# Corner blocks alone by DMA in batch 0, the division by the row sums behind the product with v, and earlier products

## The chip, the core and the metric

The kernel runs on one core of one Trainium2 chip. TensorE (PE) multiplies matrices into PSUM, VectorE (DVE) and ScalarE (ACT) work on PSUM and SBUF, GpSimd (POOL) on SBUF, and 16 DMA engines move data; nearly all transfers are issued from SyncE's queue (SP). Each engine runs its own queue in order, and semaphores hold an instruction until what it needs is there. The metric is the device time of one execution in microseconds (us), the median of three runs.

## The reference

An attention block with a threshold, followed by a feed-forward block, all in float32:

```python
# q, k, v: (8 batches, 8 heads, 576, 64)
scores = q @ k.T / 8                       # per head, 576 x 576
scores = where(scores >= rowmax - tau, scores, -1e9)
attn = exp(scores - rowmax)
attn = attn / (rowsum(attn) + 1e-9)
x = (attn @ v) -> (8*576, 8*64)            # tokens x 512
h = x @ w_in                               # 4608 x 1024
e = exp(h - rowmax); sm = e / (rowsum(e) + 1e-9)
u = h * sm
ln = (u - mean(u)) / sqrt(var(u) + 1e-6) * g_ln
out = ln @ w_out                           # 4608 x 512
```

w_in and w_out arrive as 64-bit floating-point numbers; the kernel turns their bits into float32 itself.

## The kernel before, in words

**Slots and rounds.** The attention is cut into 144 slots, 18 to a batch (PER = 18). A slot (b, kind, hp, r) is 128 query rows for each of the two heads of pair hp, against all 576 keys. Kinds 0 and 1 are the first 512 queries; kind 2 takes the last 64 queries of all pairs. Slots with r = 0 and r = 1 belong together, and such a pair of slots is a *unit* with the key (b, kind, hp): slots 2n and 2n + 1. The loop at the end of the kernel runs one round for each slot (rnd), and in each round it writes out, by hand, the order of the work for every engine. The order in which an engine gets its instructions is the order of this text.

**A slot on its way.** In round s: PE computes the scores of both heads into PSUM (`scores`, L434). VectorE finds for each head the extreme of a row and adds tau (`maxes`, L455: one custom instruction and a short read of its accumulator, twice). ScalarE turns the scores into a value that is 0 or very far from it (`ramp`, L470, out of PSUM), which sets the PSUM free for the next slot, and then takes the exponential with its row sum `sm` (`exps`, L479). In round s + 1: GpSimd computes 1/(sum + 1e-9) (`normalise`, L486 and L487) and multiplies both heads' 128x576 by it (L489); VectorE transposes both in blocks of 32x32 (`blocks`, L501) into the unit's tile T. When the second slot of a unit is transposed, DMAs carry T into a second tile wT in which the 32-row blocks stand where the product needs them (L510 and L512, or L517 for kind 2): 1152 KB in three or four transfers.

**The product with v.** Some rounds later (`pv_due`: 3 after the second slot, LAG_PV, plus 1 for slots below 6 and slots 11, 17 and 27) PE multiplies wT with v (`attend_steps`, L542, 72 matmuls, into a pair of PSUM banks taken from the two pairs p0 and p1), and `attended` copies the result into xh or xe, the tokens of the feed-forward (L572, ScalarE). A product is only started in a round with no feed-forward step on PE or with an h step.

**The feed-forward** is cut into pieces of 128 tokens. A piece has two h steps (`ff_h`, L605 with `split`, 32 matmuls each), max and exponential (L620, L629), the multiplication h * e (L635), statistics (L650 and GpSimd's L654 to L661), normalisation to V and u (L671, L676), a swap of blocks by DMA (`ff_swap`, L687), a transposition (`ff_turn`, L697) and two o steps (`ff_o`, L710, 64 matmuls each). In `ff_o` the flag `other` says which of the two PSUM banks takes which rows of w_out. At most one step of this kind runs in a round.

**Weights.** In the first 16 rounds one 128x512 piece x of the weights is made each round, x = rnd + 1: `weight_load` (DMA into a raw tile), `weight_e` on ScalarE (L263), `weight_m` on VectorE (L282 multiplies the high words by 2^-112, L286 masks and shifts the result), `weight_b` on VectorE (L308), and one round later `weight_c` on GpSimd (L332), for pieces from 8 on also `weight_f` on ScalarE (L340) and `weight_d` (DMA, L347). In a round VectorE gets `weight_b(x)` and then `weight_m(x + 1)`.

**Heads.** For batch 0, q and k of a head pair are turned by PE (`turn`, L371) and kept in SBUF by ScalarE (`keep`: L388 for k, L390 for q). `whole_pair` does so for pairs 1, 2 and 3 in rounds 0, 2 and 4; it takes both PSUM pairs p0 and p1, q in the first. The columns of kT are written in an order that puts the even keys first.

**The order in a round**, as far as the change touches it: scores, maxes, ramp and exps of slot rnd; `whole_pair`; `normalise(rnd - 1)`; the feed-forward jobs in `middle`; `weight_c`; a feed-forward step on PE; the product with v (`attend_steps`, then `attended`); `blocks(rnd - 1)`; the jobs in `late`; `weight_e`, `weight_b`, `weight_load`, `weight_m`; `weight_f`, `weight_d`; loads of q, k and v.

**Buffers.** w has four buffers, T two, wT two; raw tiles of the weights share the places of the feed-forward's tiles.

## Time and profile before

| | |
|---|---|
| median of 3 runs | 856.63 us (856.11 to 857.89) |
| the profiled execution | span 854.9 us; the profile gives no time around it |
| PE, busy share of the span | 96% |
| VectorE | 79% |
| ScalarE | 67% |
| GpSimd | 58% |
| DMA, queue q1 | 165.82 MB, 76.7% of the 16 engines' span |

A line of the timeline has the start in us, the length in us, the engine, the line of the kernel, the operation, output and input tiles, the shape (partitions x elements) and how many instructions were merged (x2); in brackets at its end stands how long the engine was idle before it, and what ended that. Consecutive instructions of an engine overlap a little, so the step from one start to the next is the better measure of what an instruction costs in its queue. A line of a group has the line, engine, operation, tiles, shape and count, then the sum of busy time, the mean length in ns, and the idle time before. Lines of DMA give the count, the size of one and the median time from issue to landing.

### The profile page before, as it was taken

How to read it: one execution, taken by the hardware profiler on the slowest of the kernel's cores; microseconds unless marked ns; L12 is line 12 of the kernel's file. 1: busy time of each engine (PE TensorE's matmuls, PEld its weight loads, DVE VectorE, ACT ScalarE, POOL GpSimd, SP SyncE). 2: the span in 40 equal slices, each digit the busy share in tenths (PEclk: the TensorE clock that was granted, in tenths of full speed). 3: DMA queues.
4: the chain of work that ended last, by engine and by line, in shares of the span. 5: the costliest groups of instructions: out<-in, count | busy, mean ns of one | idle time of the engine just before them, and what ended most of it. 6: DMA issues, size and time to landing. Idle time of an engine off the chain costs nothing.

```text
span 854.9 us, 36109 instructions
## 1 busy us (share of the span) xinstructions
PE 819.9 (96%) x15363; PEld 620.5 (73%) x15363; DVE 674.6 (79%) x1225; ACT 570.0 (67%) x1127; POOL 496.1 (58%) x945
## 2 busy tenths in 40 slices
PE   6778899999999999999999999999999999999997
PEld 5555677778677787777688877777777777777655
DVE  5997787989788888888788878888888878787361
ACT  6886876777767666667666666666677777775121
POOL 4885656666566656565566666565666655555120
PEclk8899999999999999999999999999999999999999
DMA  9999778798888888887888778887788887655212
GB/s 343 254 249 213 191 194 233 188 259 204 226 229 202 211 185 218 216 216 190 201 215 218 195 177 209 207 217 207 195 221 226 207 188 175 165 137 140 67 38 63
DMA packets 75314, 168.54 MB, mean 197 GB/s; under 512 B 11146, under 2 KB 32658, under 8 KB 75154
## 3 DMA queue, kind: packets, MB, share of 16 engines
q1 hardware_dynamic: 74866, 165.82, 76.7%
q8 instruction: 120, 1.97, 1.0%
q10 hardware_dynamic: 288, 0.43, 0.2%
q14 instruction: 40, 0.33, 0.1%
HBM read 46.14 MB, written 9.44 MB: 65 GB/s over the span
## 4 chain that ended last, share of the span: by engine, by line
PE 83%; DMA 4%; DVE 4%; ACT 3%; issue 2%; POOL 2%; SPq 1%; DVEq 0%; ACTq 0%; POOLq 0%
PE o_ps L710 27%; PE h_ps L605 22%; PE s_ps L434 15%; PE pv L542 14%; DMA wT<-T 3%; PE h_ps L595 3%; ACT w L470 1%; DVE w L455 1%; ACT w L479 1%; DVE T L501 1%; POOL w L489 1%; POOL sm L487 0%; PE s_ps L379 0%; DVE w L308 0%; PE tp L371 0%
## 5 line engine op out<-in xcount | busy, mean ns | idle before, releaser
L710 PE MATMUL o_ps<-w,uT 64*64 64x256 f32 x4608 | 269.5, 376 | 2.2 <-issue 1.6
L470 ACT ACTIVATE w<-s_ps,nth 128x576 f32<-128x576 f32 x280 | 196.8, 738 | 105.6 <-DVE nth L455 88.6
L455 DVE CUSTOM_DVE_ANT_0 w<-s_ps,tau_t 128x576 f32<-128x576 f32 x280 | 200.0, 751 | 83.5 <-PE s_ps L434 52.4
L710 PEld LDWEIGHTS o_ps<-w,uT 64*64 64x64 f32 x4608 | 221.8, 133 | 55.4 <-ACT xh L572 12.0
L489 POOL TENSOR_SCALAR w<-w,sm 128x576 f32<-128x576 f32 x288 | 220.6, 778 | 14.3
L501 DVE STREAM_TRANSPOSE T<-w 128x576 f32<-128x576 f32 x288 | 207.7, 756 | 22.6 <-POOL w L489 22.3
L605 PE MATMUL h_ps<-w,xh 64*64 64x512 f32 x1856 | 220.8, 589 | 0.0
L479 ACT ACTIVATE w<-w,ntau 128x576 f32<-128x576 f32 x288 | 219.6, 767 | 0.0
L542 PEld LDWEIGHTS pv<-wT,v 64*64 64x64 f32 x5760 | 172.6, 136 | 39.8 <-issue 16.7
L434 PE MATMUL s_ps<-kT,qT 64*64 64x512 f32 (+1 forms) x2048 | 175.8, 416 | 13.4 <-ACT w L470 11.3
L542 PE MATMUL pv<-wT,v 64*64 64x128 f32 (+1 forms) x5760 | 173.9, 263 | 8.3 <-DMA wT<-T 7.4
L605 PEld LDWEIGHTS h_ps<-w,xh 64*64 64x64 f32 x1856 | 118.4, 133 | 77.2 <-issue 43.6
L486 POOL TENSOR_SCALAR sm<-sm 128x2 f32<-128x2 f32 x144 | 34.2, 237 | 186.5 <-ACT w L479 182.8
L487 POOL TENSOR_TENSOR sm<-sm,mone 128x2 f32<-128x2 f32 x144 | 106.7, 741 | 12.0
L434 PEld LDWEIGHTS s_ps<-kT,qT 64*64 64x64 f32 x2048 | 72.7, 137 | 21.7 <-ACT w L470 16.2
L572 ACT COPY xh<-pv 128x256 f32<-128x256 f32 x64 | 25.4, 396 | 80.9 <-PE pv L542 80.9
L671 ACT ACTIVATE V<-u,nb,rs 128x1024 f32<-128x1024 f32 x36 | 44.7, 1240 | 40.5 <-POOL nb L661 33.6
L697 DVE STREAM_TRANSPOSE uT<-V 128x1024 f32<-128x1024 f32 x36 | 44.1, 1225 | 15.9 <-DMA V<-u 15.6
L479 ACT ACTIVATION_READ_ACCUMULATOR w<-w,ntau 128x1 f32 x288 | 55.4, 192 | 0.0
L676 DVE TENSOR_SCALAR u<-u,rs,nb 128x1024 f32<-128x1024 f32 x36 | 34.9, 971 | 19.5 <-ACT V L671 17.9
L635 DVE TENSOR_TENSOR u<-h_ps,u 128x1024 f32<-128x1024 f32 x36 | 42.8, 1190 | 9.4 <-ACT u L629 9.4
L620 DVE TENSOR_REDUCE hm<-h_ps 128x1 f32<-128x1024 f32 x36 | 42.9, 1193 | 4.9 <-PE h_ps L595 2.7
(77 smaller groups left out, 553.5 us busy)
## 6 DMA issues: line engine op xcount, KB each, us to landing
wT<-T SPq DMA_DIRECT2D x160, 288.0 KB, 6.5
wT<-T SPq DMA_DIRECT2D x64, 576.0 KB, 5.5
v<-in_v_dram SPq DMA_DIRECT2D x16, 576.0 KB, 6.0
V<-u SPq DMA_DIRECT2D x144, 64.0 KB, 3.5
out_dram<-ob SPq DMA_DIRECT2D x71, 128.0 KB, 2.6
q<-in_q_dram SPq DMA_DIRECT2D x28, 288.0 KB, 6.1
k<-in_k_dram SPq DMA_DIRECT2D x27, 288.0 KB, 6.4
qT<-flip SPq DMA_DIRECT2D x48, 144.0 KB, 3.2
```

The source lines that it names most:

```text
L434: nc.tensor.matmul(out=ps[h][ROWS[y], ks], lhsT=lhsT, rhs=d["kT"][ROWS[h], ks], start=True, stop=True,)
L455: nc.vector.tensor_tensor_reduce(out=w, in0=ps[:, 0:S], in1=(zero if loose else tau_t).to_broadcast([P, S]), scale=1.0, scalar=BIG, op0=AL ...
L470: nc.scalar.activation(out=d["w"][x], in_=d["w"][x] if d["loose"] else d["ps"][x][:, 0:S], func=AF.Prelu, bias=d["nth"][x], scale=-1.0, al ...
L479: nc.scalar.activation(out=w, in_=w, func=AF.Exp, bias=ntau, scale=1.0, accum_out=sm[:, x : x + 1])
L487: nc.gpsimd.tensor_tensor(out=sm, in0=sm, in1=mone, op=ALU.pow)
L489: nc.gpsimd.tensor_scalar(out=w, in0=w, scalar1=sm[:, x : x + 1], scalar2=1.0, op0=ALU.mult, op1=ALU.mult)
L501: nc.vector.transpose(out=T[:, :, r, h, :], in_=w)
L542: nc.tensor.matmul(out=to, lhsT=d["v"][ROWS[u], (h0 + h - u) % 4, m,], rhs=rhs, start=m == 0, stop=m == NK - 1,)
L605: mm = nc.tensor.matmul(out=h[ROWS[y], f], lhsT=x[ROWS[r], c, ROWS[y]], rhs=w1_parts[ROWS[r], c, part ^ r], start=part == 0 and c == 0, st ...
L671: nc.scalar.activation(out=V, in_=u, func=AF.Identity, bias=nb, scale=rs)
L697: nc.vector.transpose(out=uT, in_=d["V"].rearrange("p y (m x) -> p m y x", x=32))
L710: nc.tensor.matmul(out=d["o"][ROWS[z], 512 * (r ^ other) : 512 * (r ^ other) + 256], lhsT=d["uT"][ROWS[r], m].rearrange("p y x -> p (y x)" ...
```

## The change

Seven edits, all of which touch batch 0 or the weights:

1. **`weight_s`** (new): for pieces 4 to 10 the multiplication by 2^-112 is made by GpSimd, into the place of the finished weight, two pieces ahead (in round x - 3 for piece x); `weight_m` then only masks and shifts.
2. **`keep`**: for the head pairs of batch 0, kT keeps the keys in their own order.
3. **`normalise`**: for slots below 18 it computes 1/(sum + 1e-9) but no longer multiplies the weights by it. `sm` of these slots lives in a tile with six buffers.
4. **`corners`** (new) takes the place of `blocks` for slots below 18: VectorE transposes into T in another order of blocks, GpSimd copies the slot's share of T (128x1152) into a second tile `more` (`copy`, called behind `weight_b`), and with the second slot of a unit four DMAs of 32 partitions bring the blocks that stand in the wrong 32 rows back from `more` into T, 590 KB in all. The product then reads T.
5. **`spread`** (new): at the end of a product of batch 0, eight small matmuls against the identity write 1/sum, one value for each query column and repeated over the 64 rows of a head, into PSUM beside the product; ScalarE copies them to SBUF (`by`, in the place of `more`).
6. **`attended`**: for batch 0 two VectorE multiplications of 128x128 (product in PSUM by `by`) write the tokens; ScalarE's copy L572 falls away there.
7. **When products run**: the extra round is left out for slots 1, 3, 5 and 11; in round 18 (rnd == PER) a product may run behind an o step. In `ff_o`, `other` is off for batch 0.

The core of the diff:

```diff
+    def weight_s(x):
+        if in_bits(x):
+            hi = raws[x]["raw"].bitcast(F32).rearrange("p (n two) -> p n two", two=2)[:, :, 1]
+            dst = piece(x)[1]
+            nc.gpsimd.tensor_scalar(
+                out=dst, in0=hi, scalar1=2.0**-112, scalar2=1.0, op0=ALU.mult, op1=ALU.mult
+            )
+            raws[x]["scaled"] = dst.bitcast(I32)
...
         if nm == "k":
+            if i < NP:
+                of, to = room[:, 0 : 64 * len(ms)], pair(i)["kT"][:, 64 * ms[0] : 64 * ms[-1] + 64]
...
         nc.gpsimd.tensor_tensor(out=sm, in0=sm, in1=mone, op=ALU.pow)
+        if s < PER:
+            return
...
+    def corners(s):
...
+        T, more = [u[x].rearrange("p (c m) r h x -> p c m r h x", c=2) for x in ("T", "more")]
+        for h, w in enumerate(d["w"]):
+            nc.vector.transpose(out=T[:, :, :, r, h], in_=w.rearrange("p (m c x) -> p c m x", m=NK, c=2))
+
+        def copy():
+            of, to = [u[x][:, :, r].rearrange("p k h x -> p k (h x)") for x in ("T", "more")]
+            nc.gpsimd.tensor_copy(out=to, in_=of)
+            if r == 0:
+                return
+            of, to = [x.rearrange("p c m r h x -> p c (m r h x)") for x in (more, T)]
+            for g in range(2):
+                for half in range(2):
+                    at, src = 64 * half + 32 * (1 - g), 64 * half + 32 * g
+                    nc.sync.dma_start(out=to[at : at + 32, g], in_=of[src : src + 32, 1 - g])
+            u["wT"] = T.rearrange("p g m r h x -> p g m r h x")
+
+        return copy
...
+    def spread(key):
...
+        for r, rc in enumerate(unit["rc"]):
+            for u in range(2):
+                for h in range(2):
...
+                    nc.tensor.matmul(
+                        out=to, lhsT=rc[ROWS[u], h : h + 1].to_broadcast([64, 64]),
+                        rhs=ident[ROWS[u], ROWS[u]].rearrange("p (g x) -> p g x", g=2), start=True, stop=True,
+                    )
...
+        nc.scalar.copy(out=by, in_=y)
...
     def attended(key):
         b, kind, hp = key
+        if b == 0:
+            spread(key)
+            by = units[key]["by"]
...
-        nc.scalar.copy(out=to, in_=y)
+        if b == 0:
+            for u in range(2):
+                nc.vector.tensor_tensor(out=to[:, u], in0=y[:, u], in1=view(by)[:, u], op=ALU.mult)
+        else:
+            nc.scalar.copy(out=to, in_=y)
...
-        other = len(t) == 3 and t[2]
+        other = len(t) == 3 and t[0] > 0 and t[2]
...
+    LATE = (PER - 1, PER + 9)
+    SCALED = range(4, 11)
...
-            pv_due.append((s + LAG_PV + (s < 6 or s in (11, PER - 1, PER + 9)), (b, kind, hp)))
+            pv_due.append((s + LAG_PV + (s in LATE), (b, kind, hp)))
...
-            if due and (step is None or step[0] == "h") and len(pairs_free) > (step == ("h", 0)):
+            if due and (step is None or step[0] == "h" or rnd == PER) and len(pairs_free) > (step == ("h", 0)):
...
-            if rnd - 1 in live:
+            copied = None
+            if rnd - 1 in live and rnd - 1 < PER:
+                copied = corners(rnd - 1)
+            elif rnd - 1 in live:
                 blocks(rnd - 1)
...
                 weight_b(x)
+                if copied is not None:
+                    copied()
+                    copied = None
...
                     weight_m(x + 1)
+                if x + 2 in SCALED:
+                    weight_s(x + 2)
+            if copied is not None:
+                copied()
```

More of the change, by code (lines that the diff above doesn't have):

```diff
@@ L281, in weight_m @@
         if in_bits(x):
[L282 to L287 removed]
+            of = d.get("scaled", m)
+            if of is m:
+                nc.vector.tensor_scalar(
+                    out=m.bitcast(F32), in0=hi.bitcast(F32), scalar1=2.0**-112, scalar2=None,
+                    op0=ALU.mult,
+                )
+            nc.vector.tensor_scalar(
+                out=m, in0=of, scalar1=0x7FFFFFFF, scalar2=3,
                 op0=ALU.bitwise_and, op1=ALU.logical_shift_left,
@@ L476, in exps @@
         d = live[s]
-        d["sm"] = sm = small.tile([P, 2], F32, tag="sm", name="sm")
+        d["sm"] = sm = small.tile(
+            [P, 2], F32, tag="late" if s < PER else "sm", bufs=6 if s < PER else 3, name="sm"
+        )
         for x, w in enumerate(d["w"]):
@@ L491, in normalise @@
             )
+    def corners(s):
+        b, kind, hp, r = slots[s]
+        key = (b, kind, hp)
+        if r == 0:
+            units[key] = dict(
+                T=work.tile([P, NB, 2, 2, 32], F32, tag="T", name="T"),
+                more=work.tile([P, NB, 2, 2, 32], F32, tag="wT", bufs=2, name="wT"),
+                rc=[],
+            )
+        u = units[key]
+        d = live.pop(s)
+        u["rc"].append(d["sm"])
+        T, more = [u[x].rearrange("p (c m) r h x -> p c m r h x", c=2) for x in ("T", "more")]
[4 more added lines that the diff above has]
+            nc.gpsimd.tensor_copy(out=to, in_=of)
+            if r == 0:
+                return
[6 more added lines that the diff above has]
+        return copy
     def blocks(s):
@@ L550, in attend_steps @@
                         yield
+    def spread(key):
+        b, kind, hp = key
+        unit = units[key]
+        y = unit["y"][1].rearrange("p (u n) -> p u n", u=2)[:, :, 256:384]
+        for r, rc in enumerate(unit["rc"]):
+            for u in range(2):
+                for h in range(2):
+                    to = y[ROWS[h], u]
+                    if kind == 2:
+                        to = to.rearrange("p (r g x) -> p r g x", r=2, g=2)[:, r]
+                    else:
+                        to = to.rearrange("p (g r x) -> p r g x", r=2, g=2)[:, r]
+                    nc.tensor.matmul(
+                        out=to, lhsT=rc[ROWS[u], h : h + 1].to_broadcast([64, 64]),
+                        rhs=ident[ROWS[u], ROWS[u]].rearrange("p (g x) -> p g x", g=2), start=True, stop=True,
+                    )
+        unit["by"] = by = unit["more"].rearrange("p k r h x -> p (k r h x)")[:, 0:256].rearrange(
+            "p (u n) -> p u n", u=2
+        )
+        nc.scalar.copy(out=by, in_=y)
     def attended(key):
         b, kind, hp = key
+        if b == 0:
+            spread(key)
+            by = units[key]["by"]
         tag, y = units.pop(key)["y"]
```

11 lines of the change are left out of this document (4 added, 7 removed).

## The prediction

> **What bounds the kernel now.** I read the page, then busy time by stretches, then the engines' instructions in order of time for the first 20 of the 144 rounds. Columns of a stretch: length, busy time (and count) of each engine, granted clock, DMA share, rate.
>
> ```profile
> span 854.9 us, 36109 instructions
> PE 819.9 (96%) x15363; PEld 620.5 (73%) x15363; DVE 674.6 (79%) x1225; ACT 570.0 (67%) x1127; POOL 496.1 (58%) x945
> ...
> 70.00:77.00 7.00, 3.84 (x80) 3.60 (x84) 3.44 (x4) 0.12 (x2) 4.36 (x7) 0.80 1.05 226
> 180.00:190.00 10.00, 10.00 (x176) 8.79 (x172) 8.45 (x17) 7.10 (x15) 5.57 (x12) 1.00 1.02 269
> ```
>
> From about 120 us PE is full (10.00 of 10), and it cannot catch up there. The change touches batch 0 only, so what counts is how much earlier or later round 30 starts, where the walk of the loop gives the same work as before. Here is round 7 on VectorE. Each round opens with the first of its two L455, and I call that moment M; counting pairs from round 0 gives M7 = 42.92 and M8 = 47.31.
>
> ```profile
> 42.92 0.75 DVE L455 CUSTOM_DVE_ANT_0 w<-s_ps,tau_t 128x576 f32<-128x576 f32 x1
> ...
> 44.28 1.43 DVE L501 STREAM_TRANSPOSE T<-w 128x576 f32<-128x576 f32 x2
> 45.64 0.83 DVE L308 SCALAR_TENSOR_TENSOR w<-raw,em 128x512 int32<-128x512 int32 x1
> 46.51 0.43 DVE L282 TENSOR_SCALAR em<-raw 128x512 f32<-128x512 f32 x1
> 46.97 0.43 DVE L286 TENSOR_SCALAR em<-em 128x512 int32<-128x512 int32 x1
> 47.31 0.75 DVE L455 CUSTOM_DVE_ANT_0 w<-s_ps,tau_t 128x576 f32<-128x576 f32 x1
> ```
>
> There is no gap: in rounds 4 to 11 VectorE is the bound, at 4.39 us in this round. Its own queue is the thing to watch. ScalarE in rounds 4, 7 and 16:
>
> ```profile
> 32.34 0.72 ACT L390 ACTIVATE qT<-tp,scl 128x576 f32<-128x576 f32 x1
> ...
> 46.62 0.38 ACT L572 COPY xh<-pv 128x256 f32<-128x256 f32 x1
> ...
> 101.74 0.39 ACT L572 COPY xh<-pv 128x256 f32<-128x256 f32 x1
> ```
>
> The copy of the product with v stands behind ramp and exps of its round; in round 7 it ends at 47.00, M + 4.08. Today nobody on VectorE waits for it.
>
> The third bound is the transfer of the transposed weights in round 12: in the chain of waits 12.33 us, while VectorE and ScalarE have next to nothing to do (70 to 77 us above).
>
> ```profile
> 61.22 12.33 DMA wT<-T
> ```
>
> **The change, part by part.** Edits counted from M of the round.
>
> *VectorE waits for ScalarE.* In batch 0 the last step of a product with v is now: 8 small matmuls (spread), a ScalarE copy of 128x256 in the place of L572, then two VectorE multiplications 128x128, and these stand in VectorE's queue ahead of the two transposes, L308, L286 and the next round's L455. The ScalarE copy has the size of L572, so it ends at M + 4.08 at the earliest, +0.07 to hand over. For the multiplications:
>
> ```profile
> 118.59 0.28 DVE L388 COPY kT<-s_ps 128x128 f32<-128x128 f32 x1
> 118.80 0.54 DVE L392 TENSOR_SCALAR qT<-s_ps,scl 128x320 f32<-128x320 f32 x1
> ...
> L635 DVE TENSOR_TENSOR u<-h_ps,u 128x1024 f32<-128x1024 f32 x3 | 3.6, 1188 | 0.0
> ```
>
> One costs between 0.15 (128/1024 of L635) and 0.28 (the copy of 128x128 out of PSUM, whole); I take that copy's 0.21 from start to start, 0.42 for two.
>
> The rounds as they are now (M4, M5, M11, M12, M13, M16, M17, M18 and M20 are the L455 rows, in this order):
>
> ```profile
> 28.64 0.76 DVE L455 CUSTOM_DVE_ANT_0 w<-s_ps,tau_t 128x576 f32<-128x576 f32 x1
> ...
> 33.41 0.75 DVE L455 CUSTOM_DVE_ANT_0 w<-s_ps,tau_t 128x576 f32<-128x576 f32 x1
> ...
> 61.98 0.76 DVE L455 CUSTOM_DVE_ANT_0 w<-s_ps,tau_t 128x576 f32<-128x576 f32 x1 [0.48 <-PE s_ps L434]
> 66.38 0.76 DVE L455 CUSTOM_DVE_ANT_0 w<-s_ps,tau_t 128x576 f32<-128x576 f32 x1
> 78.37 0.76 DVE L455 CUSTOM_DVE_ANT_0 w<-s_ps,tau_t 128x576 f32<-128x576 f32 x1 [4.86 <-PE s_ps L434]
> 97.45 0.76 DVE L455 CUSTOM_DVE_ANT_0 w<-s_ps,tau_t 128x576 f32<-128x576 f32 x1 [2.51 <-PE s_ps L434]
> ...
> 100.17 1.20 DVE L697 STREAM_TRANSPOSE uT<-V 128x1024 f32<-128x1024 f32 x1
> 101.30 1.19 DVE L620 TENSOR_REDUCE hm<-h_ps 128x1 f32<-128x1024 f32 x1
> 102.41 0.74 DVE L455 CUSTOM_DVE_ANT_0 w<-s_ps,tau_t 128x576 f32<-128x576 f32 x1
> ...
> 106.88 0.76 DVE L455 CUSTOM_DVE_ANT_0 w<-s_ps,tau_t 128x576 f32<-128x576 f32 x1 [0.43 <-PE s_ps L434]
> 117.24 0.75 DVE L455 CUSTOM_DVE_ANT_0 w<-s_ps,tau_t 128x576 f32<-128x576 f32 x1
> ```
>
> So the transposes start at M + 4.57 in place of M + 1.36: +3.21 in a round with such a product. The multiplication by 2^-112 (L282), 0.46 from start to start, leaves VectorE in rounds 2 to 8. Rounds 6 and 8 become 4.39 + 3.21 - 0.46 = 7.14, round 10 (not relieved) 7.60; rounds 5 and 7 become 3.93, round 9 stays 4.39. Together 34.1 where it is 61.98 - 33.41 = 28.6: **+5.6**.
>
> *The first product moves from round 5 to round 4*, where whole_pair(3) holds both PSUM pairs.
>
> ```profile
> 33.12 2.29 PE L542 MATMUL pv<-wT,v 64*64 64x128 f32 x72 [0.79 <-ACT qT L390]
> ```
>
> It waits for the same ScalarE copy as now, which ends at M4 + 4.42 (33.06 - 28.64), but this is now a wait in VectorE's round 4: product to M + 6.8, spread 0.25 (8 of 72 matmuls of the row), copy to 7.5, multiplications to 8.0, transposes, L308 and L286 2.6, so M5 = M4 + 10.6 in place of 4.77: **+5.8**.
>
> *Corners by DMA.* 590 KB a pair of slots in place of 1152, so the 12.33 us should go. But the SyncE transfer now follows the POOL copy, which follows the late transposes, with one round less of lag.
>
> ```profile
> L489 POOL TENSOR_SCALAR w<-w,sm 128x576 f32<-128x576 f32 x44 | 32.6, 754 | 2.2
> ...
> L487 POOL TENSOR_TENSOR sm<-sm,mone 128x2 f32<-128x2 f32 x22 | 16.9, 768 | 1.8
> L332 POOL TENSOR_TENSOR w<-w,em 128x512 int32<-128x512 int32 x11 | 14.6, 1329 | 6.0 <-DVE w L308 6.0
> ...
> L486 POOL TENSOR_SCALAR sm<-sm 128x2 f32<-128x2 f32 x22 | 6.1, 276 | 22.7 <-ACT w L479 22.0
> ```
>
> By the slope from L486 to L489, 0.83 ns a column, the copy of 1152 columns takes 1.23 us (between 0.96, without the fixed part, and 1.51, as two L489). From M of the round: transposes end 6.0, copy 7.4, the fourth of four issues starts 2.2 later (0.72 each), and lands 3.6 (as V<-u, also between SBUF tiles) to 8.1 us after (as the 144 KB loads): 13.2 to 17.7.
>
> ```profile
> L517 SPq DMA_DIRECT2D wT<-T x4: 567/720/1538, 111.1 to 114.0; - x4
> k<-in_k_dram SPq DMA_DIRECT2D x8, 144.0 KB, 8.1
> V<-u SPq DMA_DIRECT2D x8, 64.0 KB, 3.6
> ```
>
> The product of two rounds later is needed at M + 12.2 (M of its round is 11.07 later, and it must start 1.1 behind that to be ready for the ScalarE copy). So each of three products comes 1.0 to 5.5 late; I take 1.0, the row of the nearest kind: **+3.0** (up to +16).
>
> *Rounds 11 to 13.*
>
> ```profile
> 66.06 3.80 PE L605 MATMUL h_ps<-w,xh 64*64 64x512 f32 x32
> ...
> 106.67 3.63 PE L710 MATMUL o_ps<-w,uT 64*64 64x256 f32 x64
> ```
>
> Round 12 loses its DMA wait. VectorE opens it later than PE has its scores, so the h there (3.44 to the next matmul) ends at M + 2.35, the product at 4.55, spread and ScalarE copy 5.2, multiplications 5.7, then transposes, L620, L308, L282, L286: 9.8 in place of 78.37 - 66.38 = 12.0: **-2.2**. Rounds 13 to 15 I count at nothing, 1 either way: a product moves from round 15 to 14, and h in rounds 13 and 14 (3.44 each) covers VectorE's wait as far as it goes.
>
> *Rounds 16 and 17.* The ScalarE copy of round 16 ends at M + 4.7 (102.13 - 97.45; two keeps stand before it), the multiplications at 5.2, then by the rows L501 1.36, L697 1.13, L620 1.11: M17 = M16 + 8.8 where it was 4.96, and o of round 17 waits for L697 as now: **+3.8**.
>
> *Round 18 with its product behind o.* o (106.67 to 110.1) to M + 3.2, product 5.4, spread, copy, multiplications 6.5, transposes 7.9, M19 at 8.1. The round of the product alone (19) falls away, but the walk of the loop shows that rounds 27, 28 and 29 then carry products alone, not just 28 and 29: one round like round 7 more, 4.4. 12.5 for 117.24 - 106.88 = 10.4: **+2.1**.
>
> *Near nothing.* Transposes no longer waiting for POOL's scaling gain some 0.3 in rounds 1 to 3, where PE's scores are as late; contiguous kT, the swapped o banks and the product of slots 16 and 17 in round 23 (PE is full there; VectorE's wait is covered by 5 us of h and v) cost 0 to 1. POOL's round: 0.28 + 0.77 + 1.33 + 1.23 + 0.7 (512 columns) = 4.3, below the new mean of 5.5. That cover gone, POOL would be the bound.
>
> VectorE against POOL: L308 takes 0.68 alone and 1.05 with POOL busy beside it.
>
> ```profile
> 41.03 1.05 DVE L308 SCALAR_TENSOR_TENSOR w<-raw,em 128x512 int32<-128x512 int32 x1
> 71.05 0.68 DVE L308 SCALAR_TENSOR_TENSOR w<-raw,em 128x512 int32<-128x512 int32 x1
> ```
>
> The Trainium skill (SBUF — State Buffer, section SBUF: two separate sides) goes further: VectorE with two SBUF inputs or in a two-port mode and GpSimd exclude each other for a whole instruction. The row agrees in kind: 0.37 of stretch. By the row the sum stays; by the rule, with 2 us more POOL work a round, some 0.4 would come on top in ten rounds, and the sum would be 4 higher.
>
> **Sum:** 5.6 + 5.8 + 3.0 - 2.2 + 3.8 + 2.1 - 0.3 = +17.8 us on a span of 854.9. The median of the runs, 856.63, lies 1.7 above that span; the same on top gives **874 us**.
>
> **The rivals.** (a) *Smaller loss:* round 4's product does not hold VectorE so long, and transfers land in time: without +5.8, +3.0 and half of +3.8 it is +7, 864. For it: small transfers, DMA less full. Against it: the keep in round 4 is in the trace. (b) *Faster:* the multiplications find their data early, VectorE gains. Rounds 4 to 10 would then cost 4.39 each, less 0.46 in the relieved ones and 0.42 more in those with a product, 29.3 for 33.3, and round 12 would lose the 4.86 of idle time: -9, 848. For it: 12.33 us of transfer, 5 MB less to move. Against it: L572's place in ScalarE's queue, 2.6 us behind the end of L455. It decides from the point where the copy ends before M + 1.4; exps would have to stand behind it. (c) *More loss:* POOL or the transfers set the pace: corners at 8.1 us to land, 4.5 later for each of three products; 888. (d) *It doesn't do what it says:* the earlier due products wait for the same data and nothing moves, 857.
>
> **Chances.** The forecast 0.5 (868 to 880), (a) 0.2, (c) 0.17, (b) 0.1, (d) 0.03. The range 859 to 886 holds the forecast, most of (a) and half of (c). Differences below 0.2% (1.7 us) can't be told from none: faster 0.1, within 0.03, slower 0.87.
>
> **What would show it.** In the changed trace VectorE idles some 2.7 us after the second L455 in rounds 6, 8 and 10, released by the new ScalarE copy; M11 stands near 76 (it is 61.98); round 4 is the longest; nothing waits 12 us for a transfer; PE's stretches from 190 us on look as before, shifted. Wrong if M11 is below 66, or VectorE's idle time in these rounds is released by PE or DMA in place of ScalarE, or the shift at round 30 is given back behind it.

## The result and the profile after

| | before | after |
|---|---|---|
| median of 4 runs each | 857.26 us (856.11 to 858.07) | 895.11 us (891.34 to 897.73) |
| ratio, 95% interval | | 1.0449 (1.0412 to 1.0486) |
| span of the profiled execution | 854.9 us | 893.6 us |

The change makes the kernel 38 us slower; 874 us was forecast. First the head of the page of the kernel after:

```profile
span 893.6 us, 36426 instructions
...
PE 833.1 (93%) x15507; PEld 621.8 (70%) x15507; DVE 679.6 (76%) x1236; ACT 570.2 (64%) x1127; POOL 497.7 (56%) x934
```

Its busy time by stretches (columns as in the prediction): rounds 5 to 10, 11 to 20, 21 to 25, and the ten microseconds from 180 on.

```profile
40.30:78.12 37.82, 24.16 (x392) 16.50 (x392) 29.41 (x57) 23.65 (x48) 26.26 (x32) 0.78 0.57 161
78.12:145.96 67.84, 57.45 (x1103) 41.44 (x1107) 48.56 (x97) 44.21 (x90) 36.26 (x57) 0.90 0.53 129
145.96:185.99 40.03, 30.77 (x563) 21.48 (x559) 22.73 (x44) 19.30 (x39) 17.68 (x35) 0.87 0.60 163
180.00:190.00 10.00, 10.00 (x160) 7.17 (x156) 9.06 (x18) 7.12 (x15) 4.07 (x9) 0.85 0.95 281
```

The same rounds of the kernel before, by the same view:

```profile
33.41:61.98 28.57, 19.69 (x388) 13.98 (x385) 27.09 (x56) 24.03 (x51) 24.61 (x33) 0.88 0.98 259
61.98:122.78 60.80, 53.60 (x1034) 39.38 (x1030) 46.98 (x88) 44.32 (x92) 37.61 (x65) 0.94 0.85 194
122.78:153.25 30.47, 28.88 (x611) 23.11 (x606) 22.61 (x43) 19.54 (x39) 18.45 (x35) 1.00 0.90 236
```

Read VectorE's busy time, the third of the five (PE, PEld, DVE, ACT, POOL). In rounds 5 to 10 it had 1.48 us of idle time (28.57 - 27.09) and now has 8.41; but it is also busy 2.3 us longer, although multiplications have been taken from it. In rounds 21 to 25, for which the forecast had 0 to 1 us, PE has fewer matmuls than before (563 for 611) and VectorE is busy as long (22.7 for 22.6), and yet they last 40.0 us in place of 30.5. The share of the DMA engines falls in all three (0.98 to 0.57 in rounds 5 to 10): the change does take load off them. The granted clock is lower in all three too (0.78 for 0.88, 0.90 for 0.94, 0.87 for 1.00); no run separates what that costs from what the waits cost. In the last row PE is full from 180 us on, as before, though at a granted clock of 0.85 (1.00 before), and nothing is made up behind it: round 26 starts 32.7 us later than before, and the end comes 38.7 us later.

VectorE in rounds 4 to 7 of the kernel after, from its timeline (start, length; in brackets the idle time before it and what ended it):

```profile
36.69 0.49 DVE L646 TENSOR_TENSOR xh<-pv,wT 128x128 f32<-128x128 f32 x2 [5.97 <-ACT wT L618]
...
40.30 0.74 DVE L468 CUSTOM_DVE_ANT_0 w<-s_ps,tau_t 128x576 f32<-128x576 f32 x1
...
44.98 0.74 DVE L468 CUSTOM_DVE_ANT_0 w<-s_ps,tau_t 128x576 f32<-128x576 f32 x1
...
48.99 0.49 DVE L646 TENSOR_TENSOR xh<-pv,wT 128x128 f32<-128x128 f32 x2 [2.58 <-ACT wT L618]
49.39 1.43 DVE L524 STREAM_TRANSPOSE T<-w 128x576 f32<-128x576 f32 x2
50.74 0.65 DVE L319 SCALAR_TENSOR_TENSOR w<-raw,em 128x512 int32<-128x512 int32 x1
51.50 1.18 DVE L288 TENSOR_SCALAR em<-w 128x512 int32<-128x512 int32 x1
52.60 0.74 DVE L468 CUSTOM_DVE_ANT_0 w<-s_ps,tau_t 128x576 f32<-128x576 f32 x1
```

The wait that was forecast is there: 2.58 us in round 6, ended by ScalarE's new copy L618, and 5.97 us in round 4. In rounds 6, 8 and 10 L618 follows exps on ScalarE without a gap, as the forecast had it; in round 6:

```profile
48.60 0.35 ACT L618 COPY wT<-pv 128x256 f32<-128x256 f32 x1
```

Over the first 205 us the view of waits gives for it (total, times, longest):

```profile
DVE xh L646 <- ACT wT L618: 25.2, 7, 6.0
DVE xe L646 <- ACT wT L618: 4.7, 1, 4.7
DVE xh L646 <- POOL nb L737: 2.2, 1, 2.2
```

That is 32.1 us in nine rounds (the third row is the same wait, put down to an instruction of GpSimd). The transfers of the corners, from the view of DMA of the first 170 us (count, size, landing):

```profile
T<-wT SPq DMA_DIRECT2D x36, 144.0 KB, 2.4
```

They land in 2.4 us, quicker than the 3.6 to 8.1 of the forecast. The products of rounds 6, 8 and 10 still begin only as they land: for round 6 the four are issued from 40.13 to 42.55 us, so by equal steps the third would land at 43.7 and the fourth at 44.4 (an estimate), and PE takes its first weights from T at 43.85 and goes on at 44.34. The view of waits puts this down to L319. It costs nothing here, because ScalarE's copy stands behind exps anyway. The 12.33 us of the chain of waits before are gone.

Where the 38.7 us of span sit, from the first L468 of a round against the first L455 before:

| stretch | before | after | difference | forecast |
|---|---|---|---|---|
| up to M4 | 28.64 | 29.29 | +0.65 | -0.3 |
| round 4 | 4.77 | 11.01 | +6.24 | +5.8 |
| rounds 5 to 10 | 28.57 | 37.82 | +9.25 | +5.6, and +3.0 for late corners |
| rounds 11 to 15 | 35.47 | 34.59 | -0.88 | -2.2 |
| rounds 16 and 17 | 9.43 | 14.25 | +4.82 | +3.8 |
| rounds 18 to 20 | 15.90 | 19.00 | +3.10 | +2.1 with the light round below |
| rounds 21 to 25 | 30.47 | 40.03 | **+9.56** | 0 to 1 |
| rounds 26 to 31 | 27.00 | 29.96 | +2.96 | the light round |
| from round 32 on | 674.65 | 677.65 | +3.00 | 0 |

The late corners stand in rounds 5 to 10, since the forecast had M11 near 76 with them. By the walk of the loop, the kernel after runs each step of the feed-forward in rounds 19 to 26 one round earlier than the kernel before, so the rows from round 18 on compare rounds with different steps. Rounds 18 to 31 together cost +15.62 us, where the forecast had +2.1 and 0 to 1.

In rounds 21 to 25 the last product of batch 0 is the matter. PE's timeline of the kernel before has it in round 21,

```profile
124.59 1.26 PE L542 MATMUL pv<-wT,v 64*64 64x64 f32 x67
```

and that of the kernel after in round 23:

```profile
164.00 1.25 PE L589 MATMUL pv<-T,v 64*64 64x64 f32 x70
```

VectorE's timeline of the kernel after:

```profile
153.69 1.44 DVE L548 STREAM_TRANSPOSE T<-w 128x576 f32<-128x576 f32 x2 [5.89 <-DMA wT<-T]
...
162.39 0.81 DVE L752 TENSOR_SCALAR u<-u,rs,nb 128x1024 f32<-128x1024 f32 x1 [0.34 <-ACT V L747]
167.90 0.49 DVE L646 TENSOR_TENSOR xe<-pv,wT 128x128 f32<-128x128 f32 x2 [4.71 <-ACT wT L618]
...
178.23 1.25 DVE L773 STREAM_TRANSPOSE uT<-V 128x1024 f32<-128x1024 f32 x1 [5.15 <-DMA V<-u]
```

SyncE's timeline of the kernel after:

```profile
151.97 0.59 SPq L168 DMA_DIRECT2D q<-in_q_dram  x1
168.46 0.60 SPq L557 DMA_DIRECT2D wT<-T  x1
169.10 2.94 SPq L559 DMA_DIRECT2D wT<-T  x2
172.09 3.37 SPq L763 DMA_DIRECT2D V<-u  x3
```

and the view of its waits, from 148 to 176 us:

```profile
SPq L557 <- DVE xe L646: 15.8, 1, 15.8
```

VectorE waits three times, 5.89, 4.71 and 5.15 us. The product of slots 16 and 17 runs two rounds later, it now reads T itself, and the copy of 1/sum (`by`) lies in a wT; both stay taken until the product, and the multiplications behind it, have run in round 23. With two T and two wT, the next batch's unit transposes into the T that a transfer is still emptying (5.89). The transfer L557 then waits 15.8 us at the head of SyncE's queue until L646 frees the wT. Behind it in that queue stands the swap V<-u (L763): its data were ready with L752 at 163.2, it is issued at 172.09, and VectorE's L773, which needs it, waits 5.15 us and holds up the next round.

### The profile page after: what moved, and what is told of

The parts are those of the page before. It is cut to its first block, busy times and chain, and to the rows that moved or that the text cites. A ratio compares the mean times of both kernels' runs of the same rounds, so it can differ in the third digit from the quotient of the medians.

```text
span 893.6 us, 36426 instructions
## 1 busy us (share of the span) xinstructions
PE 833.1 (93%) x15507; PEld 621.8 (70%) x15507; DVE 679.6 (76%) x1236; ACT 570.2 (64%) x1127; POOL 497.7 (56%) x934
## 2 busy tenths in 40 slices
DMA packets 74292, 163.27 MB, mean 183 GB/s; under 512 B 11274, under 2 KB 32786, under 8 KB 74130
## 4 chain that ended last, share of the span: by engine, by line
PE 73%; DMA 7%; DVE 6%; SPq 4%; issue 3%; ACT 2%; POOL 1%; DVEq 0%; ACTq 0%
PE o_ps L786 24%; PE h_ps L681 19%; PE pv L589 13%; PE s_ps L447 13%; DMA wT<-T 6%; PE h_ps L671 3%; SPq L763 1%; DVE T L524 1%; DVE w L468 1%; ACT w L483 1%; DVE T L548 1%; DMA V<-u 1%; SPq L559 1%; DVE w L319 0%; SPq L535 0%
## 5 line engine op out<-in xcount | busy, mean ns | idle before, releaser
L786 PEld LDWEIGHTS o_ps<-w,uT 64*64 64x64 f32 x4608 | 217.8, 134 | 70.4 <-issue 17.2
L468 DVE CUSTOM_DVE_ANT_0 w<-s_ps,tau_t 128x576 f32<-128x576 f32 x280 | 200.0, 751 | 73.0 <-PE s_ps L447 45.9
L548 DVE STREAM_TRANSPOSE T<-w 128x576 f32<-128x576 f32 x252 | 181.2, 754 | 29.7 <-POOL w L506 18.1
L447 PE MATMUL s_ps<-kT,qT 64*64 64x64 f32 (+1 forms) x2048 | 175.6, 422 | 30.1 <-ACT w L483 27.9
L506 POOL TENSOR_SCALAR w<-w,sm 128x576 f32<-128x576 f32 x252 | 193.4, 779 | 12.5
L681 PEld LDWEIGHTS h_ps<-w,xh 64*64 64x64 f32 x1856 | 120.9, 135 | 78.5 <-issue 36.6
L589 PEld LDWEIGHTS pv<-wT,v 64*64 64x64 f32 x5040 | 148.1, 134 | 32.9 <-issue 13.6
L589 PE MATMUL pv<-wT,v 64*64 64x128 f32 (+1 forms) x5040 | 149.4, 261 | 6.1 <-DMA wT<-T 4.4
L447 PEld LDWEIGHTS s_ps<-kT,qT 64*64 64x64 f32 x2048 | 70.2, 138 | 39.4 <-ACT w L483 34.6
L648 ACT COPY xh<-pv 128x256 f32<-128x256 f32 x56 | 22.1, 395 | 73.1 <-PE pv L589 73.1
L773 DVE STREAM_TRANSPOSE uT<-V 128x1024 f32<-128x1024 f32 x36 | 44.3, 1230 | 21.4 <-DMA V<-u 21.1
L705 ACT ACTIVATE u<-h_ps,hm 128x1024 f32<-128x1024 f32 x36 | 40.1, 1115 | 22.8 <-DVE hm L696 16.3
L752 DVE TENSOR_SCALAR u<-u,rs,nb 128x1024 f32<-128x1024 f32 x36 | 35.0, 972 | 18.0 <-ACT V L747 17.8
```

The costliest lines, as they stand in the source:

```text
L447: nc.tensor.matmul(out=ps[h][ROWS[y], ks], lhsT=lhsT, rhs=d["kT"][ROWS[h], ks], start=True, stop=True,)
L468: nc.vector.tensor_tensor_reduce(out=w, in0=ps[:, 0:S], in1=(zero if loose else tau_t).to_broadcast([P, S]), scale=1.0, scalar=BIG, op0=AL ...
L506: nc.gpsimd.tensor_scalar(out=w, in0=w, scalar1=sm[:, x : x + 1], scalar2=1.0, op0=ALU.mult, op1=ALU.mult)
L548: nc.vector.transpose(out=T[:, :, r, h, :], in_=w)
L589: nc.tensor.matmul(out=to, lhsT=d["v"][ROWS[u], (h0 + h - u) % 4, m,], rhs=rhs, start=m == 0, stop=m == NK - 1,)
L681: mm = nc.tensor.matmul(out=h[ROWS[y], f], lhsT=x[ROWS[r], c, ROWS[y]], rhs=w1_parts[ROWS[r], c, part ^ r], start=part == 0 and c == 0, st ...
```

## The experiments

Every kernel ran beside the kernel before on the same chip. The experiments were spread over three chips, so where two edited kernels are compared, their ratios to the kernel before count too. A shift is the start of a round less its start in the kernel before. e4 puts the larger of a product and its own copy in place of the product; the others compute what the kernel after, or before, computes.

**e1: the multiplications at the end of VectorE's round** (behind the transposes and the weights):

```diff
-            for u in range(2):
-                nc.vector.tensor_tensor(out=to[:, u], in0=y[:, u], in1=view(by)[:, u], op=ALU.mult)
+            def multiply():
+                for u in range(2):
+                    nc.vector.tensor_tensor(out=to[:, u], in0=y[:, u], in1=view(by)[:, u], op=ALU.mult)
+            return multiply
...
-                attended(attending)
+                multiply = attended(attending)
...
+            if multiply is not None:
+                multiply()
```

> The changed kernel with one edit: the two VectorE multiplications of a batch 0 product are issued at the end of VectorE's work of the round, behind the transposes and the weights, in place of ahead of them. Theory (VectorE's queue is held at its head by ScalarE's copy; idle time there sums to 32 us in the changed profile): 20 to 30 us less than the changed kernel, 865 to 875, and round 4's start to round 11's start near 36 us (48.8 in the changed kernel, 33.3 before). Rival 1 (the stretched mask L288 and the wait of round 21 for a tile T are the loss): less than 8 us gained, 887 or more. Rival 2 (the corner transfers set the pace): no gain.

875.94 us (872.79 to 879.01), ratio 1.0235 (1.0191 to 1.0278): 19 us of the 38 are gone, where 20 to 30 were expected. Shift +3.8 at round 11 (+16.1 in the kernel after) and +3.0 at round 20 (+23.1). The view of waits, first 205 us:

```profile
DVE xh L648 <- ACT wT L618: 3.5, 2, 1.9
...
DVE xh L648 <- DMA T<-wT: 2.6, 1, 2.6
```

and that of SyncE, 130 to 185 us:

```profile
SPq L557 <- DVE xe L648: 16.2, 1, 16.2
```

In the first row's place stood 25.2 us; the second is one wait that ends with a transfer of the corners. But SyncE's wait is still there, since L648 still frees the wT only in round 23, and from round 20 to round 32 the shift grows from +3.0 to +17.7. So the wait at the head of VectorE's queue is shown for rounds 4 to 20; what follows is a second thing.

**e2: the old due rounds and no product in round 18**, in the kernel after:

```diff
-            pv_due.append((s + LAG_PV + (s in LATE), (b, kind, hp)))
+            pv_due.append((s + LAG_PV + (s < 6 or s in (11, *LATE)), (b, kind, hp)))
...
-            if due and (step is None or step[0] == "h" or rnd == PER) and len(pairs_free) > (step == ("h", 0)):
+            if due and (step is None or step[0] == "h") and len(pairs_free) > (step == ("h", 0)):
```

> The changed kernel with its edit 7 undone: products fall due when they did before (an extra round for slots 1, 3, 5 and 11), and none runs behind an o step in round 18. Theory (head of the queue): round 4 loses its 6 us of idle time, the products of rounds 5, 7, 9 and 10 each still hold VectorE by 2.7, and the last product of batch 0 comes back to round 21, so that the tile T is free in time: 10 to 15 us less than the changed kernel, 880 to 885. Rival (earlier products help, the rest of the change loses): no gain or a loss, 893 or more.

878.84 us (878.77 to 883.58), ratio 1.0282 (1.024 to 1.0325), 16 us below the kernel after, where 10 to 15 were expected. Round 4 is back (shift at round 5: +0.25 for +6.9), rounds 5, 7, 9 and 10 now carry the wait (7.6 to 8.2 us each), and round 11 stands at +12.5 for +16.1: the earlier due rounds cost 3.6 there. At round 20 it is +18.8, at round 32 +20.4. Its rounds 21 to 25 add 1.8, not 9.6, and SyncE's wait for L646 doesn't occur: here the last product runs in round 21.

```profile
148.55 0.49 DVE L646 TENSOR_TENSOR xe<-pv,wT 128x128 f32<-128x128 f32 x2 [5.50 <-ACT wT L618]
```

**e3: the last product of batch 0 a round earlier due**, in the kernel after, so that T and wT come free before unit 10 wants them; it then runs in round 20:

```diff
-    LATE = (PER - 1, PER + 9)
+    LATE = (PER + 9,)
```

> The changed kernel with the last product of batch 0 (slots 16 and 17) due one round earlier, so that it runs in round 20 beside h and not in round 23. Theory (in round 21 VectorE's transposes wait 5.9 us for a DMA because T's other buffer is held until round 23, and in rounds 23 and 24 the held queue makes the swap of blocks late): 6 to 12 us less, 883 to 889, and no wait of a transposition for a DMA in round 21. Rival (PE is full there, and the lost time is made up): within 2 us of the changed kernel, 893 to 897.

891.42 us (889.17 to 895.49), ratio 1.0418 (1.0363 to 1.0472): 3.7 us less than the kernel after, where 6 to 12 were expected. The waits for T and wT are gone, and at round 26 the shift is +23.0 in place of +32.7. But from round 34 to round 41 it grows again to +35.8. VectorE there, in e3:

```profile
224.92 1.25 DVE L773 STREAM_TRANSPOSE uT<-V 128x1024 f32<-128x1024 f32 x1 [6.87 <-DMA V<-u]
```

In round 34, and in round 38 by another 5.13 us, L773 again waits for a swap. By the walk of the loop the due round also decides in which rounds the feed-forward steps run (in e3 those of rounds 30 to 37 run a round earlier); that the turn here follows its swap too closely for that reason is argued from this order, and no run moved these steps alone. So the two buffers explain where the 9.6 us sat, not why they are lost in the end.

**e4: the hand-over alone, in the kernel before**: ScalarE copies the product out of PSUM, and two VectorE instructions 128x128 read the product and the copy, at the place of the multiplications.

```diff
-        nc.scalar.copy(out=to, in_=y)
+        if b == 0:
+            by = wT[:, 0:256].rearrange("p (u n) -> p u n", u=2)
+            nc.scalar.copy(out=by, in_=y_all)
+            for u in range(2):
+                nc.vector.tensor_tensor(out=to[:, u], in0=y[:, u], in1=view(by)[:, u], op=ALU.max)
+        else:
+            nc.scalar.copy(out=to, in_=y)
```

> The kernel before with one thing added: in batch 0 ScalarE copies the product to SBUF and VectorE combines that copy with the product itself (their maximum, which is the product) in two instructions of 128x128, at the place in the queue that the multiplications have in the changed kernel. No other edit. Theory (head of the queue): the products of rounds 5, 7, 9 and 10 each cost VectorE 3.2 us, those of rounds 12 to 21 one to three each: 13 to 25 us more than before, 870 to 882. Rival (the loss comes with the corners, the POOL copy and the earlier products): 0 to 4 us more, 857 to 861.

883.38 us (882.01 to 885.78), ratio 1.0325 (1.0287 to 1.0363), above the range expected. Nothing is taken away in this kernel; two VectorE instructions are added to each product, some 0.4 us, with their wait for the copy, and it loses 26 us. Shift +15.5 at round 11, +23.2 at round 20, +24.4 at round 32. The view of waits, first 205 us:

```profile
DVE xh L578 <- ACT wT L576: 24.5, 8, 5.1
DVE xe L578 <- ACT wT L576: 5.4, 1, 5.4
```

This shows the first cause by itself: rows like those of L646 in the kernel after, without corners, without another scaling, with the old due rounds. The edit also keeps the PSUM banks and wT until VectorE has read them, which no run separates from the wait.

**e6: e1 and e3 together**, so beside e1's diff

```diff
-    LATE = (PER - 1, PER + 9)
+    LATE = (PER + 9,)
```

> The changed kernel with the multiplications behind VectorE's work of the round (as in e1) and the last product of batch 0 one round earlier (as in e3). What e1 still loses, it loses from round 21 on: 3 us at the start of round 20, 14 at round 25, 19.5 at the end. Theory (the tile T held until round 23 and the late swap behind it): the two together take 8 to 13 us off e1's 876, 863 to 868. Rival (running a round ahead only moves the waits, as e3's 4 us say): within 4 us of e1, 872 to 880.

877.19 us (875.78 to 880.05), ratio 1.022 (1.0176 to 1.0264), the same as e1, as the rival had it. Shift +8.0 at round 25 (+13.9 in e1), +20.4 at round 41. The transposes of round 21 still wait 4.96 us for a transfer out of T. As in e3, the time comes back with waits for the swap; the first 260 us:

```profile
DVE uT L775 <- DMA V<-u: 13.5, 3, 6.7
```

**e7: VectorE's weights ahead of the transposes** in the rounds with a weight piece, in the kernel after, so that GpSimd's copy (which follows the transposes) no longer runs beside L288 and L284:

```diff
-                copied = corners(rnd - 1)
+                copied = corners(rnd - 1) if rnd not in pieces else True
...
-                if copied is not None:
-                    copied()
-                    copied = None
...
+                if copied is not None:
+                    copied = corners(rnd - 1)
+                    copied()
+                    copied = None
```

> The changed kernel with one edit: in rounds 0 to 14 VectorE makes the weights (L319, L284, L288) ahead of the two transposes, so that GpSimd's copy of 1152 columns, which starts when the transposes end, runs beside L468 out of PSUM and not beside the weights. Theory (while GpSimd's copy runs, a one-input VectorE instruction on SBUF waits for it): the mask L288 is back at 0.43 us from 1.18, L284 from 1.26, and 6 to 9 us come off the changed kernel's 895: 886 to 889. Rival (L288 is long because it reads a GpSimd result): L288 stays at 1.18, time within 3 us.

893.47 us (892.79 to 901.07), ratio 1.0425 (1.0373 to 1.0477): no gain beyond the uncertainty. The groups of the first 170 us, kernel after:

```profile
L288 DVE TENSOR_SCALAR em<-w 128x512 int32<-128x512 int32 x7 | 8.3, 1179 | 0.7
L284 DVE TENSOR_SCALAR em<-raw 128x512 f32<-128x512 f32 x9 | 7.2, 797 | 6.4 <-DMA raw<-in_moe_w_in_dram 6.2
```

and of e7:

```profile
L284 DVE TENSOR_SCALAR em<-raw 128x512 f32<-128x512 f32 x9 | 4.8, 531 | 3.3 <-DMA raw<-in_moe_w_in_dram 3.1
L288 DVE TENSOR_SCALAR em<-w 128x512 int32<-128x512 int32 x7 | 3.0, 428 | 1.2 <-POOL w L302 0.5
```

The view of waits of e7, first 205 us:

```profile
DVE xh L646 <- ACT wT L618: 34.9, 8, 6.0
```

The masks fall from 1179 to 428 ns, so GpSimd's copy did stretch them. But L319 now grows, from 682 to 871 ns on average, which takes back 3.0 of the 7.7 us saved on L288 and L284; and the wait of L646 for xh is 34.9 us, where the kernel after has 27.4 (the rows of 25.2 and 2.2). In rounds 6, 8 and 10 of e7 ScalarE is idle for 1.80, 2.12 and 2.18 us right ahead of L618, where the kernel after has no gap: here the copy waits for the product. With the transposes behind the weights, GpSimd's copy and the corners go out later in their round, and these products begin 0.8 us behind M, where they began 0.6 to 1.0 us ahead of it. The view of waits names the corners for part of this:

```profile
PE pv L589 <- DMA T<-wT: 1.8, 2, 1.2
```

The products also run at a lower granted clock (0.54 for 0.68 around that of round 6). What the order gives VectorE it so loses on the way to the product.

**e8: e1, and no product in round 18**, so beside e1's diff

```diff
-            if due and (step is None or step[0] == "h" or rnd == PER) and len(pairs_free) > (step == ("h", 0)):
+            if due and (step is None or step[0] == "h") and len(pairs_free) > (step == ("h", 0)):
```

> The changed kernel with the multiplications behind VectorE's work of the round (as in e1) and no product behind the o step of round 18, so that rounds 18 to 30 carry the same steps as in the kernel before. Theory (e1's loss from round 18 on comes from the moved steps: T held until round 23, the swap issued late behind it): round 20 starts within 3 us of the kernel before and nothing is lost after: 856 to 863. Rival (the multiplications and the spread cost wherever they stand): 870 or more.

867.8 us (864.74 to 872.53), ratio 1.011 (1.0067 to 1.0154): 8 us below e1 and between the two ranges expected, and the last product runs in round 21 again (L648 for xe at 137.22, round 22 starts at 137.62; in e1 it is at 148.25, in round 23). Shift +4.1 at round 20, +10.2 at round 32 (+17.7 in e1). The wait for T is left, 7.0 us in round 21, and makes up most of the rise.

**e9: e8 and e7 together** (the diffs of e1, e8 and e7).

> e8 and e7 in one kernel: multiplications last, no product in round 18, transposes behind the weights in rounds 0 to 14. Theory (the three costs add): 4 to 7 us less than e8, 850 to 858, so perhaps faster than the kernel before. Rival (in rounds 4 to 11 ScalarE or the corner transfers, now issued later, take over as the bound): no gain over e8, or a loss of up to 5.

863.66 us (860.59 to 870.23, 12 runs), ratio 1.0087 (1.0054 to 1.0119): 4 us below e8, the intervals of the two overlap. Shift at round 11 +2.3 (+5.9 in e8), at round 13 -1.8, at round 20 +2.0, at round 32 +8.0. With VectorE's wait for xh down to 7.0 us (34.9 in e7), the new order brings round 11 forward by 3.6 us; in the medians that isn't clear of the noise, and the 850 to 858 expected were not reached.

**e10: e9, and the last product in round 20** (beside e9's the diff of e3).

> e9 with the last product of batch 0 one round earlier (round 20, beside h). In e9, round 20 starts 2 us behind the kernel before and round 22 7 us behind it: the transposes of round 21 wait 7.4 us for the DMA that empties the other tile T, as the product of slots 16 and 17 still holds the first. Theory (one tile T is held too long): that wait is gone and 4 to 6 us come off e9's 864: 857 to 861. Rival (the 5 us are those of the steps moved, and appear elsewhere): 862 or more.

863.97 us (860.83 to 865.26, 12 runs), ratio 1.0066 (1.0042 to 1.009), no gain in the median where 4 to 6 us were expected. The wait of the transposes in round 21 is shorter (7.36 us in e9), but not gone:

```profile
131.88 1.44 DVE L548 STREAM_TRANSPOSE T<-w 128x576 f32<-128x576 f32 x2 [3.55 <-POOL sm L502]
```

The view puts it down to GpSimd, but the chain of waits has the transfer wT<-T there, 7.29 us from 124.47 on. Why it is still waited for, although the product of slots 16 and 17 has read its T by 124.7, is open. The shift at round 32 is +4.4 for +8.0, but the medians of e9 and e10 can't be told apart. Unlike e3 and e6 (11 us more each), from round 32 to round 41 it loses only 1.1.

**e11: e10, and the product of slots 0 and 1 back in round 5.**

```diff
-            pv_due.append((s + LAG_PV + (s in LATE), (b, kind, hp)))
+            pv_due.append((s + LAG_PV + (s in LATE or s == 1), (b, kind, hp)))
```

> e10 with the first product (slots 0 and 1) due in round 5 again, as before. In e9 VectorE still idles 3.0 us in round 4, because that product waits for the keep of the turned queries to empty its PSUM banks, and the multiplications with it. Theory: 1 to 3 us less than e10, 855 to 859, level with the kernel before or just ahead. Rival (the tile T of round 5 must then wait for the product of round 5): the gain is given back, same as e10 or 1 to 2 more.

862.06 us (859.83 to 869.01, 12 runs), ratio 1.0059 (1.003 to 1.0087). Round 4 is as before (shift at round 5 -0.5), but round 11 stands at +3.2 (+2.7 in e10): the gain is given back, as the rival had it. This is the lowest median of the change, not to be told from e9 and e10, and it is still slower than the kernel before.

**e12: e7's order in the kernel before**, blocks behind the weights:

```diff
-            if rnd - 1 in live:
+            if rnd - 1 in live and rnd not in pieces:
                 blocks(rnd - 1)
...
+                if rnd - 1 in live:
+                    blocks(rnd - 1)
```

> The kernel before with one edit: in rounds 0 to 14 the weights stand ahead of the two transposes in VectorE's queue. Theory (the order decides who waits: the transposes no longer wait for GpSimd's scaling, 0.2 to 0.4 us every other round; VectorE is the bound in rounds 2 to 11): 1 to 3 us less than before, 854 to 856. Rival (the weights then run beside that scaling and are stretched, and the transfer of round 12, already late by 7 us, goes out later): 0 to 3 us more, 857 to 860.

860.74 us (860.31 to 870.75, 12 runs), ratio 1.0062 (1.0028 to 1.0096): slower, against my theory. Now L308 meets GpSimd. Groups in rounds 4 to 10, the kernel before:

```profile
L308 DVE SCALAR_TENSOR_TENSOR w<-raw,em 128x512 int32<-128x512 int32 x7 | 6.7, 962 | 0.0
```

and e12:

```profile
L308 DVE SCALAR_TENSOR_TENSOR w<-raw,em 128x512 int32<-128x512 int32 x7 | 10.8, 1542 | 0.0
```

One of them and GpSimd's instruction beside it, from the timeline of e12:

```profile
46.67 1.72 DVE L308 SCALAR_TENSOR_TENSOR w<-raw,em 128x512 int32<-128x512 int32 x1
...
46.57 1.27 POOL L332 TENSOR_TENSOR w<-w,em 128x512 int32<-128x512 int32 x1
```

Seven times 0.58 us make 4 of the 6.2 us by which round 11 is late; 1.1 of these stand ahead of round 4. In the kernel before the transposes stand there, which take 0.77 us on average beside GpSimd and 0.75 in e12.

## Why the forecast was right in kind and 21 us short

**Right: the wait at the head of VectorE's queue.** The forecast put the multiplications behind ScalarE's copy at the round's end and added what stands behind them. Round 4 came out at 11.0 us (10.6 forecast), round 6 at 7.62, round 8 at 7.67 (7.14), round 16 at 8.77 (8.8), round 18 at 7.93 (8.1). e4 shows the mechanism alone, e1 takes it away. M11 was to stand near 76 and stood at 78.12, but that it came so near is in part luck: the 3.0 us of late corners in it never came, and 3.7 us of longer instructions on VectorE, which the sum didn't have, stand in their place. The spread was priced as 8 of the row's 72 matmuls; the profile shows 16 at L611, of half the width, which by the same row is the same 0.25 us. "More loss by POOL or the transfers" (c), though nearest to the time measured, and "smaller loss" (a) are both off: the corners are in time for ScalarE's copy, and GpSimd is idle while it waits for the transposes.

Of the 20.9 us by which the sum fell short (17.8 for 38.7 of span), 13.5 stand in rounds 18 to 31 and 3.0 behind round 32.

**Wrong, the largest term: "the product of slots 16 and 17 in round 23 ... cost 0 to 1".** I had looked at whether VectorE's wait was covered there by h and v, and not at what the product holds until it has run. It holds a T, and its copy of 1/sum holds a wT, until round 23; in the kernel before T was free once the transfer had emptied it, and the wT with the product of round 21. Rounds 18 to 31 cost +15.62, 9.56 of it in rounds 21 to 25; in e2, with no product in round 18 and the last one in round 21, they cost +5.05. This chain of holds is read in the rows above (5.89, 15.8, 5.15). It isn't shown to be the whole reason for the wait in round 21: with the product in round 20, e6 has 4.96 us of it left and e10 3.55. What e3 and e6 add is that running this product sooner brings a gain that is lost again ten rounds later, with waits for the swap; only with the round-18 product gone as well (e2, e8, e10) does a gain stay. The product in round 18 is also what moves the last one from round 21 to 23, since e1 and e8 differ in nothing else. So the round-18 step, forecast at +2.1, is worth 8 us by medians (e1 against e8; 11 by the ratios), and together with the earlier due rounds 16 (the kernel after against e2; 14 by the ratios). How the 8 divide between the order of the feed-forward and the tiles held isn't settled.

**Wrong: "by the row the sum stays".** The relieved rounds without a product were to take 3.93 us and took 4.68. In them the 0.46 of the multiplication left VectorE, but the mask rose from 0.43 to 1.18. GpSimd's timeline in round 6 of the kernel after:

```profile
50.88 1.51 POOL L528 COPY wT<-T 128x1152 f32<-128x1152 f32 x1 [2.98 <-DVE T L524]
```

The groups of the first 170 us, kernel after:

```profile
L528 POOL COPY wT<-T 128x1152 f32<-128x1152 f32 x18 | 25.2, 1398 | 36.7 <-DVE T L524 35.4 <-ACT w L483 0.8 <-issue 0.5
...
L319 DVE SCALAR_TENSOR_TENSOR w<-raw,em 128x512 int32<-128x512 int32 x16 | 10.9, 682 | 0.1
```

and of the first 135 us, kernel before:

```profile
L308 DVE SCALAR_TENSOR_TENSOR w<-raw,em 128x512 int32<-128x512 int32 x16 | 13.7, 859 | 0.1
L282 DVE TENSOR_SCALAR em<-raw 128x512 f32<-128x512 f32 x16 | 7.3, 456 | 4.5 <-DMA raw<-in_moe_w_in_dram 4.1
```

The copy starts as the transposes end, so it is still running when L288 starts at 51.50; it ends at 52.39, and 0.89 of cover and 0.43 of work make 1.32, against 1.18 measured. The copy is stretched as well: in e7 it takes 1.14 us. I had weighed the stretch by L308 alone, 0.37, and had not laid the new copy beside the instructions that it would meet. The Trainium skill (SBUF — State Buffer, section SBUF: two separate sides) has the later of two such instructions wait until the first is done. For a mask with one input it asks for a two-port mode, which no trace shows. The sum by that rule was the better one here: 0.75 us on seven masks and 0.34 (797 less 456 ns) on nine of L284, 8.3 us of VectorE's time, less 2.8 by which sixteen of L319 became shorter (859 to 682 ns), which is 5.5 where the rule's sum had 4. In e12 the same shows on L308, 0.68 alone and 1.72 beside L332. How much of it reaches the end depends on what stands behind: nothing can be told of it in e7; in e9 round 11 starts 3.6 us earlier than in e8, and the medians differ by 4, with intervals that overlap.

**Wrong: corners late, +3.0.** They land in 2.4 us, and the products that begin with them are in time for ScalarE's copy; counted from M6, the last lands at about 11.7 (an estimate: fourth issue at 54.25, and 2.4), where 13.2 was forecast and 12.2 allowed. The nearest rows, 3.6 and 8.1, came from a kernel whose DMA engines are taken to 98% in rounds 5 to 10, and now it is 57%; that this makes the difference was not tried by itself.

**Right, and worth nothing: the relief.** The transfer's wait of round 12 is gone. Round 12 took 10.70 us (9.8 forecast, 11.99 before). In the row from 70 to 77 us the forecast read VectorE as having next to nothing to do; it is busy 3.44 of the 7 us there, and only ScalarE is idle (0.12). All in all the kernel moves 5 MB less (163.27 for 168.54 MB). In e9 the relief brings the start of round 13 1.8 us ahead of the kernel before; by round 22 it is 6.9 behind. Rival (b), 848 us, needed VectorE's rounds 5 to 10 to become shorter; even in e9 they take 28.79 us, where it was 28.57. (Its 29.3 us for rounds 4 to 10 comes out with the multiplications of two products; with all four it is 30.1.)

**Open:** 3.0 us of the shift come behind round 32, where the walk of the loop gives the same work. They aren't shown to belong to the change: e7 starts round 32 with the same shift (+35.6), has the same steps behind it and ends at +35.8, and the four executions of the kernel after differ by 6.4 us.

## What to carry to other kernels

An instruction that waits at the head of an engine's queue makes all that stands behind it late: when a step is handed from engine to engine, put the receiver behind everything that doesn't need it, which alone gave back 19 of 38 us here. When a step reads its input in place, list what it holds and until when, and follow every queue (SyncE's too) in which a transfer waits for that place. When work moves to GpSimd, lay it on the timeline beside the VectorE instructions that it will meet, and price these one by one.

## What the runs showed of the hardware that I had not expected

- A mask 128x512 on VectorE, with one input in SBUF, takes 0.43 us alone and 1.18 beside a GpSimd copy; a transposition 128x576 has 0.75 to 0.77 on average in the kernels before and after and in e12.
- GpSimd's copy 128x1152 took 1.40 us on average in the kernel after, 1.51 in the case above, and 1.14 in e7 (1.23 estimated from narrower rows of another operation).
- A transfer of 32 partitions, 144 KB, from SBUF to SBUF, one of four issued in a row, landed in 2.4 us (median of 36), with the DMA engines little more than half taken (0.57 in rounds 5 to 10).
